# Attention and a two-layer product on one core: where x is divided by its row sums, two decoding buffers, and a second decoding tied to named steps

## The chip, the cores and the metric

The kernel runs on one NeuronCore of a Trainium2 chip. The metric is device time in microseconds (us) of one execution; the shown time of a kernel is the median of its runs. TensorE (PE) multiplies matrices, VectorE (DVE) and ScalarE (ACT) work elementwise, GpSimd (POOL) reduces over partitions, and SyncE (SP) issues most of the transfers, in the order of its program: an instruction that waits on SP holds back every transfer behind it.

## The reference, cut to what matters

```python
def phi(x):                                   # q, k: 8 batches x 8 heads x 576 x 64
    proj = einsum('bhsd,df->bhsf', x, w_phi)  # 128 features
    proj = proj - max(abs(proj), axis=-1, keepdims=True)
    return concatenate([exp(proj), exp(-proj)], axis=-1)
kv  = einsum('bhsf,bhsd->bhfd', phi(k), v)
z   = sum(phi(k), axis=2)
num = einsum('bhsf,bhfd->bhsd', phi(q), kv)
den = einsum('bhsf,bhf->bhs', phi(q), z)[..., None] + 1e-06
x   = (num / den) as 4608 tokens x 512
out = ((x @ w_a) * (x @ w_b)) @ w_out         # w_a, w_b: 512x1536, w_out: 1536x512
```

All is float32. `num / den` is the division in question: one reciprocal per head and position, multiplied into the 64 columns of its head.

## The kernel before, in words

Attention goes over 32 units, a batch b (0 to 7) and a pair of heads pr (0 to 3) each, named `b_pr`. A unit is cut into steps (project, features, products, ...), and a plan spreads the steps over turns, four turns to a unit (`attention_steps`). Up to turn 40 the units run alone; there the weights of the first six slices of the hidden size are decoded beside them (`load_weights`: a packed 64-bit word becomes a high and a low float32 part; ACT makes `w` at L427, DVE shifts and adds at L430 to L440). A new `w` tile takes the buffer of the last one, alternating between two places while units run alone, and one place later.

From turn 41 on, blocks of the two-layer product run between the steps of attention (`moe_block`): 12 blocks of T1 = 384 tokens over the first six slices, so three blocks to two batches. x of a block is read as four chunks c of 128 rows, the rows of head pair c. Each is split into a high and a low part (`x_make`). The block's first output goes to DRAM (`part`). The last four blocks run after attention has ended. Beside them the rest of the weights is decoded a second time and turned into the sums that the second pass needs (`load_factors`: raw, then `w`, `w32`, the sums `ws`, the splits `wf`), and stored. Then the second pass does the other six slices with a scheme that uses seven products for eight (`FACTORS`) over 6 blocks of T2 = 768 tokens.

The order of PE's matmuls is fixed in the order of the code while attention runs (`pe`, a manual dependency from each to the next). On the other engines the order in the program is set by a scheduler that places an instruction when its own estimate says that it is ready; `issue_after` (and `behind`) puts an instruction no earlier than a named one on the same engine.

The lines around the change: `num_products` copies the numerator of a unit to `x32` (L289). `reciprocals` (L307 to L329) stores the row sums of the unit to DRAM (`den`), loads them as a 128x9 tile `r` (L315), takes the reciprocal (L317), stores that (`rec`, L319), loads it back spread over 64 partitions per head (`rb`, two transfers, L323), multiplies (L326) and stores the result (`xnorm`, L328). `x_chunk` (L500) loads a block's chunks from `xnorm`.

Of the kernel before, what the change touches and what calls it, by code (L numbers as in the profile page):

```python
# [38 lines left out]

FACTORS, AHEAD = ("w11", "w12", "s2", "s1", "s3", "w22", "s4"), 3.2  # L40
BLOCKS_LAST = 4
# [3 lines left out]
def tile_kernel(ctx, tc, qP, km, kr, vm, vr, w_phi, eye, w_a, w_b, w_out, out):  # L45
# [33 lines left out]
    rec = [dpool.tile([H, S], F32, name=f"rec{b}") for b in range(B)]  # L79
    xnorm = [dpool.tile([DM, S], F32, name=f"xnorm{b}") for b in range(B)]  # L80
    part = dpool.tile([DM, NT], F32, name="part")
# [61 lines left out]
    def split(hi, lo, src, eng_hi, eng_lo):  # L143

        (eng_hi.copy if eng_hi is nc.scalar else eng_hi.tensor_copy)(hi, src)  # L145
        eng_lo.tensor_tensor(lo, src, hi, op=ALU.subtract)  # L146

# [130 lines left out]
    def num_products(b, pr, a1, a2, consts, st):  # L278
        u = f"{b}_{pr}"
        kvh, eq = st["kvh", b, pr], st["eq", b, pr]  # L280
        pn = duo(f"pn_{u}")
        for t in range(2):
            for s in range(2):
                for j in range(2):
                    mm(pn[heads[j], t, :HALF], kvh[:, s, heads[j]], eq[:, j, s, times[t]], start=(s == 0), stop=(s == 1))
        i = b * NPAIR + pr
        place, bufs = (alone["early"], 2) if i in EARLY_X else (a2, 4)
        x32 = st["x", b, pr] = place.tile([P, S], F32, tag="x32", bufs=bufs, name=f"x32_{u}")
# [18 lines left out]
    def reciprocals(b, pr, a1, a2, st):  # L307

        n = 2 * S // P
        hs, rows = slice(2 * pr, 2 * pr + 2), slice(pr * P, (pr + 1) * P)  # L310
        one = st["dn", b, pr].rearrange("(g r) n -> g r n", r=P // 4)[:, 0]
        behind(loads, lambda: nc.sync.dma_start(den[b][hs].rearrange("h (t n) -> (h t) n", t=2), one))
        yield
        r = a2.tile([P, n], F32, tag="rec", name=f"r_{b}_{pr}")
        behind(loads, lambda: nc.sync.dma_start(r, den[b][hs].rearrange("h (a n) -> (h a) n", n=n)))  # L315
        yield
        behind(marks, lambda: nc.vector.reciprocal(r, r))  # L317
        yield
# [12 lines left out]
    def attention_steps(pools, consts, st):
# [11 lines left out]
        for i in range(B * NPAIR):  # L343
# [66 lines left out]
    def load_weights(units, a1):  # L410
# [33 lines left out]
    def load_factors(q, nm, stage, places, pool):  # L444
# [20 lines left out]
        for k, w32 in factors.items():  # L465
# [33 lines left out]

    def x_chunk(p, j, c, pool, bufs, tag="x32"):  # L500

        T, u = TS[p], f"{p}_{j}"
        x32 = pool.tile([P, T], F32, tag=tag, bufs=bufs, name=f"x32_{u}_{c}")
        t = j * T
        while t < (j + 1) * T:
            b, s0 = divmod(t, S)
            n = min(S - s0, (j + 1) * T - t)
            nc.sync.dma_start(x32[:, t - j * T : t - j * T + n], xnorm[b][c * P : (c + 1) * P, s0 : s0 + n])
            t += n
        return x32  # L510

    def x_make(p, j, c, x32, pool):
        hl = [pool.tile([P, TS[p]], F32R, tag=f"x{k}", bufs=NCC, name=f"x{k}_{p}_{j}_{c}") for k in "hl"]
        split(*hl, x32, nc.scalar, nc.vector)
        block_x.setdefault(j, {})[c] = hl

    def first_block_x():

        for c in range(NCC):
            with tc.issue_after(loads[-1].ins):  # L520
                x32 = x_chunk(0, 0, c, xpool, 2)
            yield
            with tc.issue_after(acts[-1].ins), tc.issue_after(marks[-1].ins):
                x_make(0, 0, c, x32, xpool)
            yield

    def moe_block(p, j):
        T, pool, hpool = TS[p], xpools[0], xpools[1]
        if j not in block_x:
# [15 lines left out]
        for f in range(NFS[p]):  # L545
# [38 lines left out]
        for cc in range(NCC):  # L584
            if loaded and cc < 2:
                for c in (2, 3) if cc == 0 else (0, 1):
                    x_make(p, j + 1, c, loaded[c], pool)
            outputs(cc, range(NFS[p] - 1 if cc < ahead else 0, NFS[p]))
            acc = accs[cc]
            o = hpool.tile([P, T], F32, tag="o", bufs=2, name=f"o_{p}_{j}_{cc}")  # L590
            nc.scalar.copy(o, acc)  # L591
            nc.sync.dma_start(dst[:, cc], o)
            yield

    def factors_of_x(j, pool, xs):
# [5 lines left out]
        for c in range(half):  # L601
            x32 = pool.tile([P, 2, T2], F32, tag="x32", bufs=2, name=f"x32_1_{j}_{c}")
            x[c], x[c + half] = x32[:, 0], x32[:, 1]
            t = j * T2
            while t < (j + 1) * T2:
                b, s0 = divmod(t, S)
                m, t0 = min(S - s0, (j + 1) * T2 - t), t - j * T2
                rows = xnorm[b].rearrange("(i c p) s -> p c i s", i=2, p=P)[:, c, :, s0 : s0 + m]
                load = lambda: (nc.sync if j else nc.sync).dma_start(x32[:, :, t0 : t0 + m], rows)
# [333 lines left out]
    with ExitStack() as c:  # L943
# [107 lines left out]
```

## Time and profile before

| what | us |
|---|---|
| median of 3 runs (1176.81 to 1181.11) | 1179.69 |
| profiled execution, its own time | 1176.17 |
| span of its trace | 1174.4 |
| PE busy | 1143.0 |
| DVE busy | 735.4 |
| ACT busy | 559.2 |

The span is what the trace covers, the rest of the profiled execution's time, 1.8 us, lies around it. The granted clock of TensorE is the full one, 2.4 GHz, in nearly all of the span. The shares of busy time are means over stages of different kind: units alone to about 112 us, units beside blocks to about 540 us, blocks beside the second decoding and blocks by themselves to about 770 us, then the second pass.

### The profile page before, as it was taken

To read this page: it belongs to the slowest core of one execution; us is meant where nothing else is said; L and a number is where in the kernel's file an instruction comes from. 1 tells how busy PE (TensorE), PEld (TensorE's weight loads), DVE (VectorE), ACT (ScalarE), POOL (GpSimd) and SP (SyncE) were. 2 spreads that over 40 slices of the span, in tenths; PEclk is the share of its full clock that TensorE was granted. 3 is DMA by queue.
4 is the path that set the end of the run, shared out by engine and by line. 5 is a ranking of instruction groups with operands and counts; after the bars stand their busy time and mean duration, and the time that the engine had idled before them with its cause. 6 is when DMAs were issued, how large, how long until landed. Compare 5 with 4: busy or idle time off the path is not lost.

```text
span 1174.4 us, 21007 instructions
## 1 busy us (share of the span) xinstructions
PE 1143.0 (97%) x8198; PEld 1028.1 (88%) x8198; DVE 735.4 (63%) x1359; ACT 559.2 (48%) x1050; POOL 140.0 (12%) x69
## 2 busy tenths in 40 slices
PE   8999999999999999999999999999999999999998
PEld 6666777787888788789999999999999999999998
DVE  6886886454554546453898122647687685958675
ACT  6886675454444535443555222435344353425332
POOL 4542323122121212110000000000000000000000
PEclk9999999999999999999999999999999999999999
DMA  5566654333241423224895110067695866768582
GB/s 194 178 205 202 191 170 135 102 92 119 68 145 56 124 83 106 67 83 152 292 289 193 54 55 27 23 190 270 190 323 173 277 217 221 265 193 290 175 259 83
DMA packets 103076, 191.76 MB, mean 163 GB/s; under 512 B 19520, under 2 KB 54720, under 8 KB 102976
## 3 DMA queue, kind: packets, MB, share of 16 engines
q1 hardware_dynamic: 100080, 180.84, 48.0%
q10 hardware_dynamic: 2896, 9.57, 2.5%
q8 instruction: 65, 1.06, 0.4%
q14 instruction: 35, 0.29, 0.1%
HBM read 150.75 MB, written 39.62 MB: 162 GB/s over the span
## 4 chain that ended last, share of the span: by engine, by line
PE 76%; DVE 9%; DMA 9%; ACT 3%; issue 2%; SPq 0%; DVEq 0%; ACTq 0%
PE po L782 11%; PE pa L671 10%; PE pa L105 10%; PE po L105 10%; PE pb L105 9%; PE pb L671 9%; PE kv L105 5%; PE pn L105 4%; PE pq L105 3%; DMA rb<-rec 3%; PE pd L105 2%; DMA rec<-r 2%; PE pk L105 1%; DMA x<-xnorm 1%; DMA raw_a<-in_w_a 1%
## 5 line engine op out<-in xcount | busy, mean ns | idle before, releaser
L218 POOL PARTITION_ALL_REDUCE mb<-p x64 | 139.7, 2228 | 362.8 <-ACT p L213 358.9
L105 PE MATMUL pa<-xh,w_a 128*128 128x384 f32 x576 | 162.0, 342 | 0.6 <-DVE h L560 0.4
L105 PE MATMUL pb<-xh,w_b 128*128 128x384 f32 x576 | 158.8, 337 | 2.6 <-ACT o L591 2.0
L105 PE MATMUL po<-hh,w_o 128*128 128x384 f32 x576 | 154.9, 342 | 1.4 <-ACT hh L145 0.9
L105 PEld LDWEIGHTS po<-hh,w_o 128*128 128x128 f32 x576 | 105.4, 190 | 7.9 <-issue 3.4
L105 PEld LDWEIGHTS pa<-xh,w_a 128*128 128x128 f32 x576 | 105.1, 188 | 8.2 <-issue 3.7
L105 PEld LDWEIGHTS pb<-xh,w_b 128*128 128x128 f32 x576 | 105.1, 188 | 3.5 <-ACT o L591 2.6
L105 PE MATMUL po<-hl,w_o 128*128 128x384 f32 x288 | 97.3, 338 | 2.0 <-DVE hl L146 2.0
L560 DVE TENSOR_TENSOR h<-pb,h 128x384 f32<-128x384 f32 x72 | 39.8, 552 | 92.0 <-PE pb L105 92.0
L105 PE MATMUL pb<-xl,w_b 128*128 128x384 f32 x288 | 96.8, 336 | 0.0
L105 PE MATMUL pa<-xl,w_a 128*128 128x384 f32 x288 | 96.8, 336 | 0.0
L180 DVE TENSOR_REDUCE m<-pk 128x8 f32<-128x1024 f32 x32 | 39.1, 1220 | 86.3 <-PE pk L105 86.3
L782 PE MATMUL po<-hh_s,own_o 128*128 128x384 f32 x288 | 80.1, 336 | 0.8 <-ACT u L770 0.7
L145 ACT CAST hh<-h 128x384 fp32r<-128x384 f32 x72 | 36.8, 512 | 73.7 <-DVE h L560 73.1
L105 PE MATMUL pn<-eq,kvh 128*64 128x288 f32 x512 | 67.9, 407 | 3.6 <-DVE kvh L276 3.5
L591 ACT COPY o<-po 128x384 f32<-128x384 f32 x48 | 22.5, 477 | 85.1 <-PE po L105 73.3
L105 PE MATMUL kv<-e,v 128*64 128x256 f32 x512 | 62.3, 385 | 0.7 <-ACT e L184 0.5
L105 PEld LDWEIGHTS pn<-eq,kvh 128*64 128x64 f32 x512 | 37.2, 137 | 27.9 <-ACT eq L226 2.9
L782 PE MATMUL po<-hh_w,own_o 128*128 128x384 f32 x216 | 58.9, 335 | 0.0
L559 ACT COPY h<-pa 128x384 f32<-128x384 f32 x72 | 34.2, 475 | 51.5 <-PE pa L105 48.1
L105 PEld LDWEIGHTS po<-hl,w_o 128*128 128x128 f32 x288 | 54.7, 190 | 2.2 <-DVE hl L146 2.2
L105 PE MATMUL pq<-q,w 64*128 64x288 f32 x256 | 48.1, 451 | 8.1 <-ACT p L201 7.2
(257 smaller groups left out, 2617.1 us busy)
## 6 DMA issues: line engine op xcount, KB each, us to landing
back_s<-kept_s SPq DMA_DIRECT2D x71, 512.0 KB
back_w<-kept_w SPq DMA_DIRECT2D x52, 512.0 KB
q<-in_qP SPq DMA_DIRECT2D x32, 288.0 KB
rb<-rec SPq DMA_DIRECT2D x64, 144.0 KB
xnorm<-x SPq DMA_DIRECT2D x32, 288.0 KB
part<-o SPq DMA_DIRECT2D x48, 192.0 KB
o<-part SPq DMA_DIRECT2D x24, 384.0 KB
out_x<-o SPq DMA_DIRECT2D x48, 192.0 KB
```

Source lines behind the costliest of these rows:

```text
L105: issue = lambda: nc.tensor.matmul(out, w, x, start=start, stop=stop, skip_group_check=True)
L145: (eng_hi.copy if eng_hi is nc.scalar else eng_hi.tensor_copy)(hi, src)
L180: nc.vector.tensor_reduce(out=m, in_=p, op=ALU.max, axis=AX.X, apply_absolute_value=True)
L218: nc.gpsimd.partition_all_reduce(mb, p32[:, j], P, bass_isa.ReduceOp.absmax)
L559: nc.scalar.copy(h32, pab["a"])
L560: nc.vector.tensor_tensor(h32, pab["b"], h32, op=ALU.mult)
L591: nc.scalar.copy(o, acc)
L671: in_turn(lambda: nc.tensor.matmul(acc[to][i], w_, x_, skip_group_check=True, **at), True)
L782: in_turn(lambda: nc.tensor.matmul(acc[m, to], w_, h_, skip_group_check=True, **f), False)
```

## The change

`reciprocals` ends with the store of the reciprocals. The undivided numerator is stored to `xraw` by a step of its own (`x_store`, a turn after the products). `x_chunk` loads a chunk of it and, as `rb`, the reciprocals of the same tokens; `x_scale` multiplies and stores the result to `xnorm` for the second pass, whose tensors are now one for each of its blocks. The chunks of the next block are loaded at slices 1 and 3 of a block and scaled at slices 3 and 5. The first block's chunks follow in turns (6, 9) after the end of the shortened list of turns. `w` of the first decoding has two buffers throughout. The second decoding takes 2.2 steps for each step of a block instead of 3.2, each step behind the last low part (`hl`) or output copy (`o`) of a block, and `kept` has four buffers for five.

```diff
-REC_TURNS0, REC_TURNS, X_TURNS = (1, 3, 5, 6, 8, 10, 10), (0, 1, 3, 4, 5, 6, 6), (5, 8)
-EARLY_X = (0, 2, 4)
+REC_TURNS0, REC_TURNS, X_TURNS = (1, 3, 5, 6), (0, 1, 3, 4), (6, 9)
...
-FACTORS, AHEAD = ("w11", "w12", "s2", "s1", "s3", "w22", "s4"), 3.2
+FACTORS, AHEAD = ("w11", "w12", "s2", "s1", "s3", "w22", "s4"), 2.2
...
+    def x_store(b, pr, a1, a2, consts, st):
+        behind(loads, lambda: nc.sync.dma_start(xraw[b][pr * P : (pr + 1) * P, :], st["x", b, pr]))
...
         behind(loads, lambda: nc.sync.dma_start(rec[b][hs].rearrange("h (a n) -> (h a) n", n=n), r))
-        yield
-        rb = a2.tile([P, S], F32, tag="rb", bufs=1, name=f"rb_{b}_{pr}")
-        for j in range(2):
-            behind(loads, lambda: nc.sync.dma_start(rb[heads[j]], rec[b][2 * pr + j : 2 * pr + j + 1].broadcast_to([D, S])))
-        yield
-        x32 = st["x", b, pr]
-        behind(marks, lambda: nc.vector.tensor_tensor(x32, x32, rb, op=ALU.mult))
-        yield
-        behind(loads, lambda: nc.sync.dma_start(xnorm[b][rows], x32))
         yield
...
-            place = alone["early"] if alone["turn"] < TURNS * ALONE - 8 and len(weights) % 2 else a1
-            w = place.tile([P, 2 * DM], F32, tag="w", name=f"w_{u}")
+            w = a1.tile([P, 2 * DM], F32, tag="w", bufs=2, name=f"w_{u}")
...
-                t = pool.tile([P, 2, n], F32R, tag="kept", bufs=5, name=f"wf_q{q}_{nm}_{k}")
+                t = pool.tile([P, 2, n], F32R, tag="kept", bufs=4, name=f"wf_q{q}_{nm}_{k}")
...
+    def x_chunk(j, c, pool, tag="x32"):
+
+        x32 = pool.tile([P, T1], F32, tag=tag, bufs=2, name=f"x32_0_{j}_{c}")
+        rb = xpool.tile([P, T1], F32, tag="rb", bufs=2, name=f"rb_{j}_{c}")
+        t = j * T1
+        while t < (j + 1) * T1:
             b, s0 = divmod(t, S)
...
+            nc.sync.dma_start(x32[:, t0 : t0 + n], xraw[b][c * P : (c + 1) * P, s0 : s0 + n])
+            for i in range(2):
+                one = rec[b][2 * c + i : 2 * c + i + 1, s0 : s0 + n]
+                nc.sync.dma_start(rb[heads[i], t0 : t0 + n], one.broadcast_to([D, n]))
             t += n
...
+    def x_scale(j, c, x32, rb):
+        nc.vector.tensor_tensor(x32, x32, rb, op=ALU.mult)
+        jj, t0 = divmod(j * T1, T2)
+        nc.sync.dma_start(xnorm[jj][c * P : (c + 1) * P, t0 : t0 + T1], x32)
...
-            split(hh, hl, h32, nc.scalar, nc.vector)
+            passed.append(split(hh, hl, h32, nc.scalar, nc.vector))
             hs.append((hh, hl))
-            if f == 2 and j + 1 < blocks[0]:
-                loaded = [x_chunk(p, j + 1, c, pool, 2) for c in range(2)]
+            if f == 1 and j + 1 < blocks[0]:
+                loaded = [x_chunk(j + 1, c, pool) for c in range(2)]
+            if f in (3, 5) and loaded:
+                for c in (0, 1) if f == 3 else (2, 3):
+                    x_scale(j + 1, c, *loaded[c])
             if f == 3 and loaded:
-                loaded += [x_chunk(p, j + 1, c, hpool, 2, "o") for c in range(2, NCC)]
+                loaded += [x_chunk(j + 1, c, hpool, "o") for c in range(2, NCC)]
...
             acc = accs[cc]
             o = hpool.tile([P, T], F32, tag="o", bufs=2, name=f"o_{p}_{j}_{cc}")
-            nc.scalar.copy(o, acc)
+            passed.append(nc.scalar.copy(o, acc))
...
             while due >= 1:
-                next(ahead, None)
+                with tc.issue_after(passed[-1].ins):
+                    next(ahead, None)
                 due -= 1
```

On DVE, where unit 2_1 takes the maximum of its features (`m`) and the exponents' argument (`d`); `kvh` is what PE multiplies next, and `x32` the numerator. Before:

```order
L180 TENSOR_REDUCE m_2_1_1165<-pk_2_1_1155 128x8
L181 TENSOR_TENSOR d_2_1_1164<-pk_2_1_1155,m_2_1_1165 128x1024
L317 RECIPROCAL r_1_1_1122<-r_1_1_1122 128x9
L440 TENSOR_TENSOR w_0_2_b_1087<-w_0_2_b_1057 128x512
L276 COPY kvh_1_3_1191<-pt_1_3_1187 128x384
L326 TENSOR_TENSOR x32_1_0_831<-x32_1_0_831,rb_1_0_1147 128x576
L219 TENSOR_TENSOR p32_2_1_1150<-p32_2_1_1150,mb_2_1_0_1175 128x576
```

And now:

```order
L180 TENSOR_REDUCE m_2_1_1179<-pk_2_1_1169 128x8
L507 TENSOR_TENSOR x32_0_1_0_1643<-x32_0_1_0_1643,rb_1_0_1644 128x384
L181 TENSOR_TENSOR d_2_1_1178<-pk_2_1_1169,m_2_1_1179 128x1024
L318 RECIPROCAL r_1_1_1131<-r_1_1_1131 128x9
L431 TENSOR_TENSOR w_0_2_b_1094<-w_0_2_b_1070 128x512
L276 COPY kvh_1_3_1205<-pt_1_3_1201 128x384
L507 TENSOR_TENSOR x32_0_0_3_1159<-x32_0_0_3_1159,rb_0_3_1160 128x384
L219 TENSOR_TENSOR p32_2_1_1164<-p32_2_1_1164,mb_2_1_0_1189 128x576
```

The multiply of unit 1_0 stood behind `kvh` of unit 1_3. Now the multiply of block 1's chunk 0 (`x32_0_1_0`, half of whose tokens are unit 1_0's) stands ahead of `d_2_1` and of that `kvh`. The next one, of chunk 1, stands right ahead of `m_2_2`.

On SP at the same place, from the store of the reciprocals of unit 1_0 to the loads that its multiply needs (`r` are the row sums as loaded, `den` as stored). Before:

```order
L319 DMA rec1_77<-r_1_0_985 128x9
L328 DMA xnorm0_84<-x32_0_3_699 128x576
L508 DMA x32_0_0_2_1126<-xnorm0_84 128x384
L168 DMA rv_2_2_1251<-in_vr 128x256
L323 DMA rb_1_0_1147<-rec1_77 64x576 x2
L312 DMA den1_69<-dn_1_2_1139 4x288
```

And now:

```order
L320 DMA rec1_77<-r_1_0_995 128x9
L316 DMA r_1_1_1131<-den1_69 128x9
L509 DMA xnorm0_92<-x32_0_0_2_1019 128x384
L168 DMA rv_2_2_1257<-in_vr 128x256
L502 DMA rb_1_0_1644<-rec0_76 64x192 x2
L502 DMA rb_1_0_1644<-rec1_77 64x192
L290 DMA xraw1_85<-x32_1_2_1105 128x576
L499 DMA x32_0_1_0_1643<-xraw0_84 128x192
L499 DMA x32_0_1_0_1643<-xraw1_85 128x192
L313 DMA den1_69<-dn_1_2_1150 4x288
L502 DMA rb_1_0_1644<-rec1_77 64x192
```

Two loads of `rb` have become four, and between the two that read `rec1` stand a store, two loads and the store of the next unit's row sums.

On DVE beside block 7, between its slices 1 and 2 (`h32` a product of a slice, `hl` its low part; names with `q` are the second decoding). Before:

```order
L560 TENSOR_TENSOR h32_0_7_1_6171<-pb_0_7_1_6158,h32_0_7_1_6171 128x384
L461 TENSOR_TENSOR ws_q1_b_6991<-ws_q1_b_6991,w32_q1_b_6908 128x256
L462 TENSOR_TENSOR ws_q1_b_6991<-w32_q1_b_6908,ws_q1_b_6991 128x256
L390 TENSOR_SCALAR w_q2_a_0_7105<-w_q2_a_0_7105 128x512
L146 TENSOR_TENSOR hl_0_7_1_6175<-h32_0_7_1_6171,hh_0_7_1_6174 128x384
L392 TENSOR_SCALAR w_q2_a_0_7105<-w_q2_a_0_7105 128x512
L146 TENSOR_TENSOR wf_q1_b_s2_7043<-ws_q1_b_6991,wf_q1_b_s2_7043 128x256
```

And now:

```order
L562 TENSOR_TENSOR h32_0_7_1_6233<-pb_0_7_1_6220,h32_0_7_1_6233 128x384
L146 TENSOR_TENSOR hl_0_7_1_6237<-h32_0_7_1_6233,hh_0_7_1_6236 128x384
L562 TENSOR_TENSOR h32_0_7_2_6276<-pb_0_7_2_6263,h32_0_7_2_6276 128x384
L146 TENSOR_TENSOR hl_0_7_2_6280<-h32_0_7_2_6276,hh_0_7_2_6279 128x384
L562 TENSOR_TENSOR h32_0_7_3_6309<-pb_0_7_3_6296,h32_0_7_3_6309 128x384
```

The instructions of the second decoding that follow the last slice of block 6, 7, 8, 9, 10 and 11, and so stand beside the outputs of that block or the next block's slices, number 62 in block 6, 56 in 7, 20 in 8, none in 9, 1 in 10 and 29 in 11 before, counted from the first slice of each, and 0, 0, 40, 41, 40 and 49 now.

## Rows read from the trace of the kernel before

**Rows 1.** The page: busy time, share, instructions; then the chain that ended last.
```profile
PE 1143.0 (97%) x8198; PEld 1028.1 (88%) x8198; DVE 735.4 (63%) x1359; ACT 559.2 (48%) x1050; POOL 140.0 (12%) x69
...
PE 76%; DVE 9%; DMA 9%; ACT 3%; issue 2%; SPq 0%; DVEq 0%; ACTq 0%
```

**Rows 2.** Windows: stretch, length, then busy time and instructions of each engine.
```profile
120.00:200.00 80.00, 73.90 (x725) 57.86 (x725) 62.15 (x104) 51.11 (x82) 22.00 (x10) 0.98 0.55 166
200.00:540.00 340.00, 335.84 (x2569) 279.37 (x2566) 169.24 (x263) 163.49 (x266) 69.18 (x32) 1.00 0.32 96
540.00:640.00 100.00, 96.30 (x544) 93.65 (x543) 83.67 (x194) 51.24 (x121) 0.00 (x0) 1.00 0.76 251
640.00:770.00 130.00, 129.34 (x746) 129.05 (x746) 42.92 (x93) 40.92 (x91) 0.00 (x0) 1.00 0.17 53
```

**Rows 3.** Waits of PE, 60 to 125 us: total us, times, longest.
```profile
PE pn L105 <- DVE kvh L276: 3.2, 4, 1.1
PE pt L274 <- ACT dn L300: 1.1, 1, 1.1
```

**Rows 4.** Line L326, the multiply: its instructions; what ended the idle time before them.
```profile
L326 DVE TENSOR_TENSOR x<-x,rb x32: 696/748/1685, 49.7 to 541.6; 128x576 f32<-128x576 f32 x32
...
  DMA rb<-rec: 20.1, 9
```

**Rows 5.** Chain of waits, 60 to 110 us: start, us, what.
```profile
61.76 5.92 DMA rec<-r
...
72.59 3.90 DMA rec<-r
...
77.05 3.94 DMA rb<-rec
...
82.94 5.17 DMA rec<-r
...
88.68 2.93 DMA rb<-rec
```

**Rows 6.** Timeline of DVE, 76 to 106 us: start, us, instruction, idle before and releaser.
```profile
79.60 0.20 DVE L317 RECIPROCAL r<-r 128x9 f32<-128x9 f32 x1
81.08 0.76 DVE L326 TENSOR_TENSOR x<-x,rb 128x576 f32<-128x576 f32 x1 [1.27 <-DMA rb<-rec]
...
86.81 1.23 DVE L181 TENSOR_TENSOR d<-pk,m 128x1024 f32<-128x1024 f32 x1
...
88.62 0.55 DVE L276 COPY kvh<-pt 128x384 f32<-128x384 f32 x1
91.63 0.76 DVE L326 TENSOR_TENSOR x<-x,rb 128x576 f32<-128x576 f32 x1 [2.46 <-DMA rb<-rec]
...
96.24 1.22 DVE L180 TENSOR_REDUCE m<-pk 128x8 f32<-128x1024 f32 x1
...
98.63 0.55 DVE L276 COPY kvh<-pt 128x384 f32<-128x384 f32 x1
```

**Rows 7.** Timeline of PE, 144 to 153 us.
```profile
148.94 0.76 PE L105 MATMUL pq<-q,w 64*128 64x288 f32 x4 [3.08 <-ACT p L201]
```

**Rows 8.** Timelines of ACT, 144 to 153 us and 176 to 184 us.
```profile
146.19 0.66 ACT L427 ACTIVATE w_o<-raw_o 128x512 f32<-128x512 f32 x1 [2.24 <-DVE w_b L440]
...
148.26 0.63 ACT L201 COPY p<-pq 128x576 f32<-128x576 f32 x1
...
180.78 0.66 ACT L427 ACTIVATE w_o<-raw_o 128x512 f32<-128x512 f32 x1 [1.86 <-DVE w_o L440]
```

**Rows 9.** Waits of DVE, 200 to 540 us.
```profile
DVE m L180 <- PE pk L105: 74.1, 11, 9.7
```

**Rows 10.** Waits of PE, 200 to 540 us.
```profile
PE po L105 <- DVE hl L146: 2.0, 1, 2.0
```

**Rows 11.** Chain of waits, 540 to 640 us.
```profile
544.63 3.41 DMA raw_a<-in_w_a
...
568.59 2.05 DMA x<-xnorm
```

**Rows 12.** Waits of ACT, 540 to 640 us.
```profile
ACT w_q_a L389 <- DMA raw_a<-in_w_a: 9.5, 3, 5.4
```

More of the change, by code (lines that the diff above doesn't have):

```diff
@@ L79, in tile_kernel @@
     rec = [dpool.tile([H, S], F32, name=f"rec{b}") for b in range(B)]
-    xnorm = [dpool.tile([DM, S], F32, name=f"xnorm{b}") for b in range(B)]
+    xraw = [dpool.tile([DM, S], F32, name=f"xraw{b}") for b in range(B)]
+    xnorm = [dpool.tile([DM, T2], F32, name=f"xnorm{j}") for j in range(NT // T2)]
     part = dpool.tile([DM, NT], F32, name="part")
@@ L145, in split @@
         (eng_hi.copy if eng_hi is nc.scalar else eng_hi.tensor_copy)(hi, src)
-        eng_lo.tensor_tensor(lo, src, hi, op=ALU.subtract)
+        return eng_lo.tensor_tensor(lo, src, hi, op=ALU.subtract)
     heads = [slice(j * D, (j + 1) * D) for j in range(2)]
@@ L285, in num_products @@
                     mm(pn[heads[j], t, :HALF], kvh[:, s, heads[j]], eq[:, j, s, times[t]], start=(s == 0), stop=(s == 1))
-        i = b * NPAIR + pr
-        place, bufs = (alone["early"], 2) if i in EARLY_X else (a2, 4)
-        x32 = st["x", b, pr] = place.tile([P, S], F32, tag="x32", bufs=bufs, name=f"x32_{u}")
+        x32 = st["x", b, pr] = a2.tile([P, S], F32, tag="x32", name=f"x32_{u}")
         nc.scalar.copy(x32.rearrange("p (t n) -> p t n", t=2), pn[:, :, :HALF])
+    def x_store(b, pr, a1, a2, consts, st):
+        behind(loads, lambda: nc.sync.dma_start(xraw[b][pr * P : (pr + 1) * P, :], st["x", b, pr]))
     def den_products(b, pr, a1, a2, consts, st):
@@ L309, in reciprocals @@
         n = 2 * S // P
-        hs, rows = slice(2 * pr, 2 * pr + 2), slice(pr * P, (pr + 1) * P)
+        hs = slice(2 * pr, 2 * pr + 2)
         one = st["dn", b, pr].rearrange("(g r) n -> g r n", r=P // 4)[:, 0]
@@ L352, in attention_steps @@
             units = ((project, 0), (q_features, TURNS), (turned_kv, 0), (summed, 0), (kv_products, 0), (num_products, 0), (z_products, 0), (kv_out, 0))
-            units += ((den_products, 0), (load_kq, -5), (load_v, -2 if i else 0))
+            units += ((den_products, 0), (load_kq, -5), (load_v, -2 if i else 0), (x_store, at["num_products"] + 1))
             for order, (f, t) in enumerate(units):
@@ L358, in attention_steps @@
             done = t0 + at["den_products"]
-            plan(10, reciprocals(b, pr, *pools, st), [done + t for t in rec_turns])
+            plan(len(units), reciprocals(b, pr, *pools, st), [done + t for t in rec_turns])
             if b == 0:
-                plan(11, x_first, [done + rec_turns[-1] + t for t in X_TURNS])
+                plan(len(units) + 1, x_first, [done + rec_turns[-1] + t for t in X_TURNS])
             if pr == NPAIR - 1:
-                plan(12, b, [done + rec_turns[-1]])
+                plan(len(units) + 2, b, [done + rec_turns[-1]])
         stages.sort(key=lambda x: x[:3])
@@ L498, in weight, with x_make @@
         return weights[key][:, i]
[L500 to L505, printed above, removed]
-            b, s0 = divmod(t, S)
-            n = min(S - s0, (j + 1) * T - t)
-            nc.sync.dma_start(x32[:, t - j * T : t - j * T + n], xnorm[b][c * P : (c + 1) * P, s0 : s0 + n])
-            t += n
-        return x32
-    def x_make(p, j, c, x32, pool):
-        hl = [pool.tile([P, TS[p]], F32R, tag=f"x{k}", bufs=NCC, name=f"x{k}_{p}_{j}_{c}") for k in "hl"]
+    def x_chunk(j, c, pool, tag="x32"):
[3 more added lines that the diff above has]
+        while t < (j + 1) * T1:
+            b, s0 = divmod(t, S)
+            n, t0 = min(S - s0, (j + 1) * T1 - t), t - j * T1
+            nc.sync.dma_start(x32[:, t0 : t0 + n], xraw[b][c * P : (c + 1) * P, s0 : s0 + n])
+            for i in range(2):
+                one = rec[b][2 * c + i : 2 * c + i + 1, s0 : s0 + n]
+                nc.sync.dma_start(rb[heads[i], t0 : t0 + n], one.broadcast_to([D, n]))
+            t += n
+        return x32, rb
+    def x_scale(j, c, x32, rb):
+        nc.vector.tensor_tensor(x32, x32, rb, op=ALU.mult)
+        jj, t0 = divmod(j * T1, T2)
+        nc.sync.dma_start(xnorm[jj][c * P : (c + 1) * P, t0 : t0 + T1], x32)
+    def x_make(j, c, x32):
+        hl = [xpool.tile([P, T1], F32R, tag=f"x{k}", bufs=NCC, name=f"x{k}_0_{j}_{c}") for k in "hl"]
         split(*hl, x32, nc.scalar, nc.vector)
@@ L520, in first_block_x @@
             with tc.issue_after(loads[-1].ins):
-                x32 = x_chunk(0, 0, c, xpool, 2)
+                chunk = x_chunk(0, c, xpool)
             yield
             with tc.issue_after(acts[-1].ins), tc.issue_after(marks[-1].ins):
-                x_make(0, 0, c, x32, xpool)
+                x_scale(0, c, *chunk)
+                x_make(0, c, chunk[0])
             yield
@@ L530, in moe_block @@
             with tc.issue_after(loads[-1].ins):
-                chunks = deque(x_chunk(p, j, c, pool, 2) for c in range(2))
+                chunks = deque(x_chunk(j, c, pool) for c in range(2))
             yield
@@ L586, in moe_block @@
                 for c in (2, 3) if cc == 0 else (0, 1):
[L587 removed]
+                    x_make(j + 1, c, loaded[c][0])
             outputs(cc, range(NFS[p] - 1 if cc < ahead else 0, NFS[p]))
@@ L603, in factors_of_x @@
             x[c], x[c + half] = x32[:, 0], x32[:, 1]
[L604 to L609, printed above, removed]
+            for t in range(0, T2, T2 // 2):
+                rows = xnorm[j].rearrange("(i c p) s -> p c i s", i=2, p=P)[:, c, :, t : t + T2 // 2]
+                load = lambda: nc.sync.dma_start(x32[:, :, t : t + T2 // 2], rows)
                 behind(feeds, load) if j else load()
-                t += m
                 yield
@@ L881, in home @@
         return wpool, f"w_{f}_{nm}"
-    kept, begun, feeds = {}, set(), []
+    kept, begun, feeds, passed = {}, set(), [], []
     weights, pools_moe, xpools, block_x, blocks, marks, acts, copies, loads, alone = {}, [], [xpool], {}, [0], [], [], [], [], dict(turn=0)
```

6 lines of the change are left out of this document (4 added, 2 removed).

## The prediction

> **What bounds the kernel now.** I read the page first, to see which engine is nearly always busy: PE, with 1143.0 of 1174.4 us [rows 1]. What a change can win is therefore the 31 us in which PE stands still, and what it can lose is new standstill. The shares of the chain that ended last say the same (76% PE, 9% DVE, 9% DMA). Next come the windows [rows 2]: each stage has its own loss. From 640 to 770 us, blocks by themselves, 746 matmuls take 130 us, 0.1743 us each; from 540 to 640 us, beside the second decoding, only 544 run in 100 us, which at that pace need 94.8 us, so 5.2 us are lost there. The second pass is touched only in how it loads x, so I leave it at its present time. Then the waits of PE by stage: near the end of the units alone it waits 3.2 us for the copy `kvh` on DVE and 1.1 us for `dn` on ACT [rows 3]; between 125 and 200 us it waits twice for a copy of p on ACT, 6.0 us together, of which one is 3.08 us [rows 7]. Last I asked who holds DVE: the multiply by `rb` has 20.1 us of idle time before it, in 9 waits for DMA [rows 4], and the chain from 61.8 us on runs through the store of `rec` and the load of `rb` [rows 5].
>
> The sum is made against the profiled execution, 1176.17 us. It lies 3.5 us under the median of the runs shown, 1179.69 us, and the forecast adds that back. What a measurement of this kernel can tell from no change I take as 0.5%, 5.9 us: below 1173.8 us is faster, above 1185.6 us slower.
>
> **Part 1, the division moves from the unit to the block.** DVE's own work hardly changes: 32 multiplies of 0.748 us (median) go [rows 4], 48 over 384 columns come, which by their columns take 0.50 us each: 23.9 against 24.0 us. SP gets 107 more transfers. They are off the path except where SP itself waits, which is what matters here. In the order DVE's multiply of block 1's chunk 0 now stands ahead of `d_2_1`, and of the `kvh` that PE stalls for already. It needs `rec1` of unit 1_0, so the store and load that the change takes out of the unit come back here. Working from the rows: before, the waits at 81.08 and 91.63 us cost DVE 1.27 and 2.46 us [rows 6]. Without the first, and with 1.0 us won already at the wait before it (PE's longest stall for `kvh` is 1.1 us [rows 3]), the reciprocal at 79.60 comes at about 78.6 and its store goes out at about 79. The store takes 3.9 to 5.9 us to land, 5.0 in the mean of three [rows 5], so SP goes on at 84. Between the two loads that read it stand four issues of about half a microsecond, so the second goes out at 86 and lands 2.9 to 3.9 us later [rows 5], at about 89.3. DVE reaches the multiply at about 85.3 (`d` at 86.81 before, 1.5 us earlier now): it waits 4.0 us. Then 0.5 for the multiply, 1.2 for `d` and 0.8 for what stands between bring `kvh` to 91.8 us instead of 88.62 [rows 6], 3.2 us late. What is queued behind this wait is what PE needs next, `kvh` of unit 1_3, and `d`, which ACT waits for. The second multiply, chunk 1 ahead of `m_2_2`: from 91.8 on DVE has 0.55 of `kvh`, 0.5 of a multiply and the 3.9 us of work that lay between the end of the multiply at 92.4 and `m` at 96.24 [rows 6], so it is there at 96.8; the reciprocal it needs comes behind `d` at 91.0, its store lands at 96.1, two issues and 3.5 us more make 100.4: a wait of 3.6 us. With multiply, `m` and `d` (3.0 us) `kvh` of unit 2_0 starts at 103.4, against 98.63 before: 4.8 us late. What goes in return is the stall for `dn` behind the last of these waits, 1.1 us [rows 3]. **+3.7 us.** If both legs are at their shortest each wait is 1.6 us less: about +0.5. With the longest they are about 1 us more: +5.7. If DVE's slack swallows both, the stalls of rows 3 go: −4.3.
>
> The Trainium skill, DMA: Bandwidth & Descriptors, section Anatomy of one DMA, puts a small transfer at a fixed part of about 2.0 us, fitted on transfers that GpSimd issues. By that price, an estimate, the two legs would be 4 us and neither multiply would wait, and this part would be −4.3 and the whole sum 8 us lower. The trace disagrees for the 4.5 KB store at this place, with 3.90 to 5.92 us.
>
> Later blocks' multiplies stand where their units ended longer ago, so they wait only for the chunk's own loads, 2.05 us for a chunk of x and up to 3.94 for `rb` by the nearest rows [rows 5, 11]. DVE has idle time there, 74.1 us before `m` from 200 to 540 us, up to 9.7 at once [rows 9], and PE loses little in that stage now: 335.84 of 340 us busy [rows 2]. But a late `hl` has cost PE 2.0 us once [rows 10]. From 0 to 5 us; nearer to the row of idle time: **+1.5 us.**
>
> **Part 2, two buffers for `w`.** ACT makes the next `w` only when DVE has added up the last: it stands 2.24 us at 146.19 and 1.86 us at 180.78, and the copy of p that PE waits for is behind it, at 148.26 in the first case [rows 7, 8]. With a second buffer both go; what is late next is PE's own last product for that copy. **−4.1 us**, between 0 (the next cast waits for DVE in its place) and −6.0 (both stalls whole).
>
> **Part 3, the second decoding.** Counted in the order it leaves blocks 6 and 7 (62 and 56 instructions on DVE) and stands with 40, 41, 40 and 49 in blocks 8 to 11. A block has 216 matmuls, 37.6 us. At DVE's mean in 540 to 640 us, 83.67 / 194 = 0.43 us [rows 2], a block of 41, with its own 12 for `h32` and `hl` and 8 for x, is 61 x 0.43 = 26 us, 70% of the block; before, DVE was busy for 84% of this stage. PE's loss of 5.2 us should fall to about 2: **−3.2 us**, between −5.2 and +2. Block 11 now has 49, 26 of them after its last slice, beside 72 matmuls of outputs (12.5 us): 11.2 us of DVE. It fits narrowly, with ACT's casts and the loads of raw words beside it: **+1.5 us**, 0 to 6. The four buffers for five of `kept` lie beside the same work and are in these bounds.
>
> One row moves the other way: on ACT the first two `w` of the second decoding now stand ahead of the output copy `o` of block 5, chunk 3, and wait for a load of raw words. Such a load takes 3.41 us in the chain, and ACT waited for it 9.5 us in 3 waits, up to 5.4 [rows 11, 12]. Behind it on ACT stand the copies that free PE's accumulators. 0 to 5.4; the load is issued well ahead, so **+1.0 us.**
>
> **Sum:** +3.7 +1.5 −4.1 −3.2 +1.5 +1.0 = +0.4 us, so 1176.6 us on the profiled scale and 1180 us on the median's.
>
> **The rivals.** A, the waits are simply gone: DVE's slack hides both early multiplies, later ones never wait, and what rows 3, 4 and 7 show is won. −4.3, −4.1 and, for the second decoding with block 11 fitting, −3.7: −12.1 us, 1168 us. For it: DVE is only 63% busy. Against: PE stalls for `kvh` already, behind the very waits that come back. By the Trainium skill's price for a small transfer, above, this is the outcome; the rows speak against its price, not against slack.
>
> B, the multiply that waits stands in DVE's order ahead of what PE needs. Alone it costs +5.7, and beside the blocks a third of the 20 to 24 later multiplies cost PE 1 us each, +7; with −4.1, −3.2, +1.5 and +1.0 as above that is +7.9: 1188 us. For it: three of the stage's present stalls are of this make, and the loads of a chunk are issued late behind SP's own waits. Against: 74.1 us of idle time. It decides from about 4.8 us of new waiting of PE: that is what the other parts win, and from 10.7 us the slowdown can be told.
>
> C, the second decoding comes too late: block 11's sums and their stores are not ready when the second pass wants them. +6 there, and −1 instead of −3.2 before: +7.1, 1187 us. For it: the rows of block 11 fill its last part to nine tenths. Against: 62 instructions stood behind block 6 before at a loss of only a few microseconds.
>
> **How the numbers follow.** The forecast, no change that can be told, 0.38; A 0.32; B 0.20; C 0.10. So faster 0.32, same 0.38, slower 0.30. The forecast's own range is 1174 to 1186 us. The range for 8 in 10 reaches to A's and past B's time: 1167 to 1190 us; its lower end is 12.7 us under the median, with parts 1 and 2 both at their best.
>
> **What would show it.** The multiply at L507 waits about 4 us for `rb` at 85 us and again at 97 us, and `kvh` of unit 2_0 is late by 4 to 5 us (if it comes early, A). PE's stalls of 3 us for p near 149 and 183 us are gone or under 1 us. Between 540 us and the second pass PE's pace is 112 or more matmuls in 20 us in every window. PE's waits from 200 to 540 us stay under 6 us in sum; over 10, B. The forecast is wrong if the alone stage comes out ahead of before, or if DVE or ACT hold the outputs of block 11 for more than 4 us.

## The result and the profile after

The changed kernel takes 1188.64 us (1187.46 to 1192.29, 6 runs) against 1179.47 us beside it: a ratio of 1.0083, 95% interval 1.0063 to 1.0103. It is slower by 9.2 us. The profiled execution's span went from 1174.4 to 1185.9 us. In the page of the changed kernel PE is busy for 2.8 us more than before [rows 1]; most of what grew is the time around it:

```profile
PE 1145.8 (97%) x8198; PEld 1028.8 (87%) x8198; DVE 746.9 (63%) x1375; ACT 560.1 (47%) x1050; POOL 139.4 (12%) x69
```

The order of PE's products is nearly the same in both kernels, so the start of the same product in two traces says how far one has fallen behind. The table gives it for the changed kernel and for those of the next section: us later than before (less than zero: ahead). Each column is one execution, and that of the kernel before took 3.3 us less than its median.

| place (start in the trace of before) | changed | hold1 | hold_all | hold_w1 | undo2 | undo3 | b_part3 |
|---|---|---|---|---|---|---|---|
| pn of unit 1_2 (79.0) | -1.9 | -1.5 | -1.3 | -1.1 | -1.1 | -0.9 | 0.3 |
| pn of unit 2_0 (99.3) | 8.6 | -2.2 | -2.0 | -1.9 | 8.3 | 7.6 | 0.6 |
| block 0 (111.7) | 10.9 | 1.6 | 3.0 | -2.1 | 9.4 | 10.1 | 0.9 |
| pn of unit 7_0 (472.5) | 17.3 | 7.5 | 2.0 | -5.2 | 11.5 | 17.8 | 3.1 |
| block 9 (652.8) | 12.8 | 3.0 | -3.4 | -10.6 | 7.0 | 19.8 | -3.2 |
| end of the last product (1170.5) | 11.9 | 2.6 | -4.9 | -13.0 | 7.4 | 23.2 | -2.9 |

So 10.9 us are lost before block 0, some 6 more beside the blocks, and 5 to 6 come back beside the second decoding. The first loss is in the waits of PE from 60 to 125 us, where [rows 3] had 3.2 and 1.1:

```profile
PE pn L105 <- DVE kvh L276: 10.7, 3, 7.1
PE pt L274 <- ACT dn L301: 1.8, 1, 1.8
```

DVE's timeline of the changed kernel, 76 to 112 us, answers to [rows 6]. The two early multiplies (L507) wait 5.54 and 4.28 us, and `kvh` starts at 92.72 and 107.26 where it started at 88.62 and 98.63. The releasers in the brackets are the last to come by the profile; the load of `k` was issued behind the last load of `rb`.

```profile
90.44 0.56 DVE L507 TENSOR_TENSOR x<-x,rb 128x384 f32<-128x384 f32 x1 [5.54 <-DMA k<-in_km]
...
92.72 0.55 DVE L276 COPY kvh<-pt 128x384 f32<-128x384 f32 x1
...
98.75 0.69 DVE L429 TENSOR_TENSOR w_a<-w_a 128x512 f32<-128x512 f32 x1 [1.96 <-ACT w_a L426]
...
104.39 0.56 DVE L507 TENSOR_TENSOR x<-x,rb 128x384 f32<-128x384 f32 x1 [4.28 <-DMA x<-xraw]
...
107.26 0.55 DVE L276 COPY kvh<-pt 128x384 f32<-128x384 f32 x1
```

On SP the store of `rec` went out at 79.18. The two loads of `rb` that went out from 82.65 on read the reciprocals of batch 0; SP had stood there 1.5 us for the load of `q`. The third, which reads what the store wrote, went out at 84.37, 5.2 us behind it, and the last that the first multiply needs at 87.15, behind a store, two loads and a store. The row of 84.37 and the wait come from views of their own:

```profile
79.18 0.38 SPq L320 DMA_DIRECT2D rec<-r  x1
...
82.65 2.17 SPq L502 DMA_DIRECT2D rb<-rec  x3
84.92 0.59 SPq L290 DMA_DIRECT2D xraw<-x  x1
85.60 0.93 SPq L499 DMA_DIRECT2D x<-xraw  x2
86.58 0.52 SPq L313 DMA_DIRECT2D den<-dn  x1
87.15 0.45 SPq L502 DMA_DIRECT2D rb<-rec  x1
```
```profile
84.37 0.45 SPq L502 DMA_DIRECT2D rb<-rec  x1
...
SPq L502 <- DMA q<-in_qP: 1.5, 1, 1.5
```

The windows of the same stretch show a second price, in the column after POOL's, the granted clock: after PE has stood for most of 86 to 93 us it runs at 0.50, 1.2 GHz, for 4 us, and the 16 products of `pn` take 4.11 us. Before, `pn` took 2.16 (the last row).

```profile
86.00:93.00 7.00, 0.32 (x4) 0.00 (x0) 2.56 (x5) 1.17 (x2) 2.58 (x2) 0.84 0.57 169
93.00:95.00 2.00, 1.59 (x8) 0.97 (x10) 1.64 (x4) 2.00 (x4) 0.00 (x0) 0.50 0.85 231
95.00:97.00 2.00, 2.00 (x12) 0.94 (x8) 1.75 (x4) 0.13 (x1) 0.00 (x0) 0.50 0.83 280
```
```profile
93.41 4.11 PE L105 MATMUL pn<-eq,kvh 128*64 128x288 f32 x16 [7.09 <-DVE kvh L276]
...
107.95 3.75 PE L105 MATMUL pn<-eq,kvh 128*64 128x288 f32 x16 [3.14 <-DVE kvh L276]
```
```profile
89.31 2.16 PE L105 MATMUL pn<-eq,kvh 128*64 128x288 f32 x16 [1.06 <-DVE kvh L276]
```

Over the whole kernel the multiply's line has this idle time before it, where [rows 4] had 20.1 for `rb`; some of it lies where DVE had nothing else to do:

```profile
L507 DVE TENSOR_TENSOR x<-x,rb x48: 543/558/1734, 61.0 to 719.0; 128x384 f32<-128x384 f32 x48
...
  DMA x<-xraw: 50.5, 19
```

PE's waits from 125 to 215 us are 2.3 us for p in three, where the kernel before had 6.0 in two, one of them [rows 7], but there is a new one of 3.2 for DVE's sums of `w`. From 558 to 658 us, the stretch that answers to the third row of [rows 2], PE runs 579 matmuls, and 746 in the 130 us behind:

```profile
PE po L105 <- DVE w_o L431: 3.2, 1, 3.2
PE pq L105 <- ACT p L201: 2.3, 3, 2.0
```
```profile
558.00:658.00 100.00, 100.00 (x579) 100.00 (x578) 37.78 (x77) 31.79 (x67) 0.00 (x0) 1.00 0.33 107
658.00:788.00 130.00, 129.34 (x746) 129.05 (x745) 101.35 (x231) 62.34 (x148) 0.00 (x0) 1.00 0.64 216
```

### The profile page after: what moved, and what is told of

Read it like the earlier page. It is cut to its first block, busy times and chain, and to the rows that moved or that the text cites. A ratio compares the mean times of both kernels' runs of the same rounds, so it can differ in the third digit from the quotient of the medians.

```text
span 1185.9 us, 21181 instructions
## 1 busy us (share of the span) xinstructions
PE 1145.8 (97%) x8198; PEld 1028.8 (87%) x8198; DVE 746.9 (63%) x1375; ACT 560.1 (47%) x1050; POOL 139.4 (12%) x69
## 4 chain that ended last, share of the span: by engine, by line
PE 75%; DVE 7%; DMA 4%; ACT 1%; issue 1%; SPq 0%; ACTq 0%; DVEq 0%
PE pa L105 12%; PE po L105 12%; PE pb L105 12%; PE po L783 10%; PE pa L672 9%; PE pb L672 8%; PE kv L105 5%; PE pn L105 3%; PE pd L105 2%; PE pq L105 2%; DMA back_s<-kept_s 1%; DMA x<-xnorm 1%; PE pk L105 1%; DVE top L684 1%; DMA rec<-r 1%
## 5 line engine op out<-in xcount | busy, mean ns | idle before, releaser
L507 DVE TENSOR_TENSOR x<-x,rb 128x384 f32<-128x384 f32 x48 | 29.6, 622 | 98.5 <-DMA x<-xraw 50.5
L105 PE MATMUL pn<-eq,kvh 128*64 128x288 f32 x512 | 71.5, 423 | 12.0 <-DVE kvh L276 11.9
L105 PE MATMUL kv<-e,v 128*64 128x256 f32 x512 | 65.0, 398 | 2.1 <-ACT e L184 2.1
L105 PEld LDWEIGHTS kv<-e,v 128*64 128x64 f32 x512 | 35.0, 141 | 24.2 <-issue 7.4
```

Source lines behind the costliest of these rows:

```text
L105: issue = lambda: nc.tensor.matmul(out, w, x, start=start, stop=stop, skip_group_check=True)
```

## The experiments

Theory D: the multiply stands too early in DVE's order. Its rival S: SP's longer queue holds everything up. Theory P3 and its rival N are on the second decoding, W on the second buffer of `w`, K on the clock. Each time is a median, with the ratio to the kernel before on the same chip. Each edit is scheduled anew, so other rows can move with the one that it names; where that bears on a reading, it is said.

**hold1, hold_all: the multiplies held where the code has them**, those of block 1, then of all blocks.

```diff
                 for c in (0, 1) if f == 3 else (2, 3):
-                    x_scale(j + 1, c, *loaded[c])
+                    with tc.issue_after(passed[-1].ins) if j == 0 else nullcontext():   # hold_all: always
+                        x_scale(j + 1, c, *loaded[c])
```

> The changed kernel with the four multiplies of block 1's chunks held behind the low part (hl) of the slice that they stand behind in the code; all transfers stay where they are. Theory D (the multiply stands in DVE's order ahead of kvh and waits there for rec and rb): the drift of 10.5 us between units 1_2 and 2_0 goes, PE reaches block 0 no later than before, and the time is 1174 to 1179 us. Rival S (SP: 107 more transfers and the waits between them hold back every load): the transfers are unchanged, so the time stays at 1186 to 1190 us.

> As the run before, with the multiplies of all blocks held so. Theory D: a further 3 to 7 us, the drift between 120 and 510 us, so 1169 to 1175 us. Rival S: 1186 to 1190 us.

1178.86 us (1.001, 0.9988 to 1.0031) and 1171.09 us (0.9945, 0.9925 to 0.9965). Both times are as D has it. The early multiplies cost 9.8 us by the medians, 8.6 by the ratios, the later ones 7.8. In the table the drift at unit 2_0 turns from +8.6 to -2.2. Against S stands the first wait: up to the load of `q` that follows the last load of `rb`, SP issues the same transfers in the same order in hold1, and `pn` of unit 1_3 behind it starts 1.4 us earlier than before, where it started 4.1 us later in the changed kernel. Further on hold1 moves transfers too, since loads of `rb` and stores to `xnorm` wait for the held multiplies, and there the two theories are not parted.

What the later multiplies cost is not all waiting for their loads. Of the 5.5 us between hold1 and hold_all at unit 7_0, 4.6 come at one place. In hold1 `hl` stands on DVE behind four splits (`xl`) of the next block's x, PE waits 1.96 us for it, and then the clock falls and `kv` takes 3.68 us. In hold_all the multiplies, and so these splits, come behind `hl`, and the wait is 0.15. First hold1, then hold_all:

```profile
394.60 1.02 DVE L146 TENSOR_TENSOR xl<-x,xh 128x384 fp32r<-128x384 f32 x2
395.54 0.55 DVE L146 TENSOR_TENSOR hl<-h,hh 128x384 fp32r<-128x384 f32 x1
...
396.14 0.69 PE L105 MATMUL po<-hl,w_o 128*128 128x384 f32 x1 [1.96 <-DVE hl L146]
...
397.08 3.68 PE L105 MATMUL kv<-e,v 128*64 128x256 f32 x16
```
```profile
392.73 0.56 DVE L146 TENSOR_TENSOR hl<-h,hh 128x384 fp32r<-128x384 f32 x1
393.21 1.02 DVE L507 TENSOR_TENSOR x<-x,rb 128x384 f32<-128x384 f32 x2
...
393.35 0.45 PE L105 MATMUL po<-hl,w_o 128*128 128x384 f32 x1 [0.15 <-DVE hl L146]
```

The kernel before has the same wait for `hl` [rows 10]. So with this wait hold_all wins something that the change had not lost.

**undo3, b_part3: the second decoding as before in the changed kernel; as now in the kernel before.**

```diff
-FACTORS, AHEAD = ("w11", "w12", "s2", "s1", "s3", "w22", "s4"), 2.2
+FACTORS, AHEAD = ("w11", "w12", "s2", "s1", "s3", "w22", "s4"), 3.2
...
-                with tc.issue_after(passed[-1].ins):
-                    next(ahead, None)
+                next(ahead, None)
```

> The changed kernel with 3.2 steps of the second decoding to a step of a block and not behind named steps, as in the kernel before. Theory P3 (spreading the second decoding over four blocks wins the 6 us by which PE catches up from 540 us on): 1193 to 1196 us, and PE falls short of its pace after block 5 again. Rival N (what is caught up there comes from elsewhere, the decoding being hidden either way): 1187 to 1190 us.

> The kernel before with only the second decoding changed: 2.2 steps behind the named steps, four buffers of kept. Theory P3: 6 us faster than before, 1172 to 1175 us. Rival N: 1178 to 1181 us.

1197.39 us (1.0162, 1.0122 to 1.0202), 1.4 us over the expected range, and 1175.34 us (0.9975, 0.9953 to 0.9997), 0.3 us over it and 2.7 under N's. P3 stands by the table between unit 7_0 and block 9. undo3 loses a further 3.4 us behind block 9, which the kernel before does not; it keeps the four buffers of `kept`, and whether they are why was not tested. The windows, undo3 first, then b_part3: 530 matmuls in 100 us against 579.

```profile
557.00:657.00 100.00, 93.74 (x530) 91.29 (x530) 80.50 (x185) 47.26 (x111) 0.00 (x0) 1.00 0.80 269
```
```profile
540.00:640.00 100.00, 100.00 (x579) 100.00 (x578) 31.45 (x63) 30.70 (x65) 0.00 (x0) 1.00 0.22 74
```

In b_part3 the 6.3 us won between unit 7_0 and block 9 stand against 3.1 lost before that. Of these 2.8 are lost at one place, behind a wait for `hl` of 1.95 us that the kernel before has too (1.96, [rows 10]); there the clock stayed at 1.00, here it fell. First the kernel before, then b_part3:

```profile
391.94 1.95 PE L105 MATMUL kv<-e,v 128*64 128x256 f32 x16
...
390.00:395.00 5.00, 3.60 (x30) 2.34 (x32) 2.79 (x5) 0.48 (x1) 0.00 (x0) 1.00 0.38 124
```
```profile
391.72 0.69 PE L105 MATMUL po<-hl,w_o 128*128 128x384 f32 x1 [1.95 <-DVE hl L146]
...
392.66 3.68 PE L105 MATMUL kv<-e,v 128*64 128x256 f32 x16
...
390.00:395.00 5.00, 3.28 (x14) 1.90 (x16) 3.12 (x6) 0.48 (x1) 0.00 (x0) 0.57 0.36 118
```

At the same wait the changed kernel loses 1.7 us and undo2 nothing. So up to 2.8 us of a column of the table can hang on whether the clock falls there; what decides it no run shows.

**hold_w1, hold_prelu, undo2, hold_w1_prelu: the second buffer of `w`.** hold_w1 and undo2 give it up in hold_all and in the changed kernel. The prelu kernels keep ACT's first step of every decoding behind the copies of kv and dn.

```diff
-            w = a1.tile([P, 2 * DM], F32, tag="w", bufs=2, name=f"w_{u}")
+            place = alone["early"] if alone["turn"] < TURNS * ALONE - 8 and len(weights) % 2 else a1
+            w = place.tile([P, 2 * DM], F32, tag="w", name=f"w_{u}")
...
-        nc.scalar.copy(back, st["kv", b, pr])
+        copies.append(nc.scalar.copy(back, st["kv", b, pr]))   # prelu; dn likewise
...
-            with tc.issue_after(acts[-1].ins):
+            with tc.issue_after(acts[-1].ins), tc.issue_after(copies[-1].ins) if copies else nullcontext():   # prelu
```

> hold_all with the first decoding's w as before (one buffer, alternating places while the units run alone). Theory W0 (two buffers trade ACT's wait for DVE's last addition against a wait for the raw words, so they win next to nothing): 1169 to 1173 us beside hold_all's 1171.1; PE's two waits for p near 145 and 180 us come back, and its wait of 4.5 us for dn near 106 us goes. Rival W4 (the 4 us of part 2 are really won): 1174 to 1177 us.

> hold_all with ACT's first step of a decoding (the one that waits for raw words) held behind the last copies of kv and dn in the code. Theory W0: what stands behind ACT's wait for raw words at 101 to 104 us is dn, which PE wants; held behind it, PE's 4.5 us wait for dn goes and the time is 1166 to 1169 us. Rival: PE waits there for something else that is as late (DVE's kvh or the cast), 1170 to 1173 us.

> The changed kernel with w of the first decoding as before, the early multiplies left where they are. Theory W (the second buffer lets ACT take the next raw words ahead of back and dn, where it waits for their load; it cost 7 us beside the held multiplies): 1180 to 1185 us, and PE's wait for dn before block 0 is under 1 us. Rival W4 (with the multiplies in the way the second buffer pays, since DVE's sums come late there): 1190 to 1194 us, and PE's two waits for p of 3 us are back.

> hold_w1 with ACT's first step of a decoding behind the last copies of kv and dn. Theory W: that step no longer stands ahead of dn with one buffer, so this changes little: 1162 to 1166 us. Rival (its 2.0 us wait for raw words near 104 us still costs PE): 1160 to 1162 us.

hold_w1 1164.11 us (0.988, 0.9863 to 0.9896), hold_prelu 1166.48 us (0.9894, 0.9875 to 0.9912), undo2 1182.11 us (1.0029, 1.001 to 1.0049), hold_w1_prelu 1164.68 us (0.9889, 0.987 to 0.9909). hold_w1 lies 5 us under the range of either theory: the second buffer does not win little, as W0 had it, but costs 7.0 us beside the held multiplies and 6.5 beside the early ones. ACT's and PE's timelines of hold_all show how most of it comes there:

```profile
104.12 0.66 ACT L418 ACTIVATE w_a<-raw_a 128x512 f32<-128x512 f32 x1 [3.04 <-DMA raw_a<-in_w_a]
...
105.57 0.50 ACT L301 ACTIVATE dn<-pd,eps 128x288 f32<-128x288 f32 x1
```
```profile
106.12 0.55 PE L274 MATMUL pt<-ident,back 128*128 128x128 f32 x3 [4.53 <-ACT dn L301]
```

With a free buffer ACT's step was placed ahead of `back` and `dn`, and waits there for raw words. In hold_w1 the same step stands behind `dn`, and PE's wait there is 0.91 us:

```profile
102.69 0.55 PE L274 MATMUL pt<-ident,back 128*128 128x128 f32 x3 [0.91 <-ACT dn L301]
```

hold_prelu's edit holds only such steps, though DVE's order moves with them, and wins 4.6 of the 7.0 us. With one buffer the same hold wins nothing. In the table 5.1 us of the buffer's price beside the held multiplies lie ahead of block 0. Beside the early ones only 1.5 of 5.8 at unit 7_0 do, and 1.7 are the clock at the wait for `hl`; how the rest comes was not followed.

**rb_old: no round trip of the reciprocals for block 1.**

```diff
-                one = rec[b][2 * c + i : 2 * c + i + 1, s0 : s0 + n]
+                one = rec[0 if j == 1 else b][2 * c + i : 2 * c + i + 1, s0 : s0 + n]
```

> The changed kernel with the reciprocals of block 1 all read from batch 0's tensor, which was written long before; every instruction of DVE up to the two early multiplies and every transfer stays at its place, but nothing waits for the store of rec of units 1_0 to 1_3 any more (half of block 1 is then divided by the wrong sums). Theory D-rt (the round trip of the reciprocals through DRAM is the wait of both multiplies): the wait of 5.5 us is under 1.5 us, the wait of 4.3 us under 2 us, the time 1179 to 1183 us. Rival D-x (the chunk's own numerators, stored and loaded again, come as late): both waits stay over 3 us, 1186 to 1190 us.

1184.02 us (1.0047, 1.0032 to 1.0062), 4.6 us faster, between the two. The waits fell from 5.54 and 4.28 to 3.53 and 3.28:

```profile
89.07 0.56 DVE L507 TENSOR_TENSOR x<-x,rb 128x384 f32<-128x384 f32 x1 [3.53 <-DMA rb<-rec]
...
102.03 1.67 DVE L507 TENSOR_TENSOR x<-x,rb 128x384 f32<-128x384 f32 x1 [3.28 <-issue]
```

The landing of `rec` is at least 1 to 2 us of each; before the second, SP still stood 1.8 us for that store, at its store of the numerators:

```profile
SPq L290 <- DMA rec<-r: 1.8, 1, 1.8
```

The rest is SP's own row of issues: with nothing to wait for in `rec`, the first of its three loads went out at 80.67 and the last that the first multiply needs still at 86.07, behind the store and loads of numerators. So S has a part in the wait, but only because a multiply stands where the wait is felt.

**rb_one, hold_w1_rb1: one transfer for both heads.**

```diff
-            for i in range(2):
-                one = rec[b][2 * c + i : 2 * c + i + 1, s0 : s0 + n]
-                nc.sync.dma_start(rb[heads[i], t0 : t0 + n], one.broadcast_to([D, n]))
+            both = rec[b][2 * c : 2 * c + 2, s0 : s0 + n].unsqueeze(1).broadcast_to([2, D, n])
+            nc.sync.dma_start(rb[:, t0 : t0 + n], both)
```

> The changed kernel with one transfer for both heads' reciprocals of a piece instead of two, 28 fewer rows on SP; the early multiplies still stand ahead of kvh. Theory D (place on DVE): at most 3 us faster, 1185 to 1189 us, since the multiply still waits for rec to land. Rival S (SP's queue): 1179 to 1184 us.

> hold_w1 with one transfer for both heads' reciprocals. Theory D: the multiplies are behind their data already, so fewer transfers win nothing: 1162 to 1166 us. Rival S: SP's transfers still hold PE up beside the blocks, 1158 to 1161 us.

1236.84 us (1.0507, 1.0485 to 1.0529) and 1226.3 us (1.0415, 1.039 to 1.0441): neither theory, and no test of S. The transfer itself is slow. hold_w1_rb1's chain of waits from 540 us on has it at 10.15 us, and while it moves, the share of busy DMA engines and GB/s (the last two columns) are:

```profile
573.16 10.15 DMA rb<-rec
```
```profile
575.00:577.00 2.00, 2.00 (x14) 2.00 (x13) 0.44 (x1) 0.00 (x0) 0.00 (x0) 1.00 0.09 31
577.00:579.00 2.00, 2.00 (x13) 2.00 (x13) 0.78 (x3) 0.51 (x1) 0.00 (x0) 1.00 0.14 47
```

**fill1: PE kept at work in its longest wait.**

```diff
         pn = duo(f"pn_{u}")
+        for n_ in range({(1, 3): 40}.get((b, pr), 0)):
+            mm(pn[heads[n_ % 2], 0, :HALF], consts[1][:, heads[n_ % 2]], eq[:, 0, 0, times[0]])
```

> The changed kernel with 40 more matmuls (64 columns of the identity against eq) written into the accumulator pn of unit 1_3 just before its own first product overwrites them, so that PE works through most of its 7.1 us wait for kvh; they need 5.4 us at the pace of that product. Theory K (the wait costs more than its length: after it PE runs at 1.2 GHz, and the 16 products of pn take 4.11 us instead of 2.16): the granted clock stays at 1.0, these 16 take 2.2 us, unit 2_0's product starts about 2 us earlier than in the changed kernel, and the time is 1186 to 1188 us. Rival (the slow products are due to late weights, not to the clock): they take 4 us again, and the time stays at 1188 to 1190 us.

1191.29 us (1.01, 1.0076 to 1.0123): slower than expected by either, though not clear of the changed kernel. The rows that it was made for are clear. The fill took 9.87 us, not 5.4, and so overran the wait, but the clock stayed at 1.00 and the 16 products of `pn` took 2.11 us instead of 4.11:

```profile
87.29 9.87 PE L105 MATMUL pn<-eq,ident 128*64 128x288 f32 x80
96.99 2.11 PE L105 MATMUL pn<-eq,kvh 128*64 128x288 f32 x16
...
106.20 2.11 PE L105 MATMUL pn<-eq,kvh 128*64 128x288 f32 x16
...
115.09 0.90 PE L274 MATMUL pt<-ident,back 128*128 128x128 f32 x3 [4.58 <-ACT dn L303]
115.92 3.68 PE L105 MATMUL kv<-e,v 128*64 128x256 f32 x16
```

So the slow products are the clock's, as K has it. That unit 2_0's product came 1.75 us earlier is not shown to be: `pn` of unit 1_3 ended 1.6 us later than in the changed kernel. What came earlier is the second multiply, by 2.46 us, and SP's order ahead of it had changed with the edit: the store of unit 1_3's numerators stands ahead of the loads of `xraw` in the changed kernel and behind them in fill1. This run does not part that from the clock. First the changed kernel, then fill1:

```profile
98.54 0.42 SPq L290 DMA_DIRECT2D xraw<-x  x1
```
```profile
104.12 0.54 SPq L292 DMA_DIRECT2D xraw<-x  x1
```

The wait of 4.58 us for `dn` ended 0.6 us earlier than that of 1.80 in the changed kernel, but behind it the clock fell (`kv` 3.68 us where 1.95 is usual), and block 0 started 2.2 us later than there.

## Why the prediction was right or wrong

The measured time lies in the range, and near rival B's 1188 us; the forecast itself, no change at 1180 us, was wrong. By its steps:

- **The early multiplies, +3.7 predicted.** The mechanism was right: place, wait and what is queued behind. DVE arrived at 84.9 (85.3 said) and waited 5.54 (4.0); the second waited 4.28 (3.6). What failed is the size: by hold1 they cost 9.3 us at block 0, of the 10.9 there. Two things were left out of the term. The clock: the two slow `pn` took 2.0 and 1.6 us more than 2.16 each. And `dn`, which I had counted as a stall that goes: it grew to 1.8 us, beside the second buffer of part 2 (0.6 in undo2). The 1.96 us before L429, where ACT's cast stood behind the copy of the late `pn`, cost nothing of their own: DVE then stood 4.28 us at the second multiply.
- **The later multiplies, +1.5 (0 to 5).** 7.8 us by hold1 against hold_all (5.5 of them by unit 7_0 in the table). I took DVE's idle time before `m` as cover. B's price of +7 there was near, but its mechanism is not shown for most of it: 4.6 us are the wait for `hl` behind the splits of x and the clock behind that, a wait that the kernel before has as well.
- **The second buffer, -4.1 (0 to -6).** The sign was wrong: 6.5 to 7.0 us lost. The step that failed is "with a second buffer both go; what is late next is PE's own last product". Late next was the load of raw words, and the scheduler placed the step that waits for it ahead of `back` and `dn`. Nor did p need the buffer: in hold_w1, with one, PE's waits for p from 125 to 215 us are 2.1 us in sum.
- **The second decoding, -3.2 +1.5 +1.0.** 5.9 us won (18.7 us behind at block 6, 12.8 at block 9), and no loss in block 11: 746 matmuls in 130 us. Block 5 loses 1.4 us, but as much in undo3, where the second decoding is as before, so the cost I added for its `o` is not seen either. The costs did not come; C falls.
- **A**'s 12.1 us were to be had, but not by its terms: hold_w1 wins 14.6 with the multiplies held and one buffer of `w`. The mean granted clock goes with it, 0.999 to 1.000 in hold_w1's runs, 0.992 to 0.997 in the kernel before beside them, 0.990 to 0.993 in the changed kernel. That DVE is 63% busy over the span said nothing on the rows where it waited.

That B's total was hit is partly chance: its terms alone (+5.7) and for the second buffer (-4.1) were too good, that for the second decoding (-0.7 in sum) too bad.

The Trainium skill's fixed part of about 2.0 us (DMA: Bandwidth & Descriptors, Anatomy of one DMA) stays below what the changed kernel shows for the store of `rec`, 5.2 us from its issue to that of the load that reads it. I had counted 5.0. But by rb_old the landing was the smaller part of the first wait.

The best kernel here is hold_w1: the division in the block, its multiplies held behind the slice they belong to, one buffer of `w`, the second decoding spread. It is 24.5 us under the changed kernel and 14.6 us under the one before.

## What to carry to other kernels

When an operation moves to where a scheduler may place it freely, look where it lands in the engine's order: if it stands ahead of the critical rows with data that must make a round trip, those rows wait with it, whatever the engine's busy share. A freed buffer lets an instruction be placed earlier as well as run earlier; ask what it waits for then, and who is behind it. Hold a moved operation behind a named row of its own stage before judging the move. And before a gain is put down to an edit, look whether the kernel before has the same wait, and whether the clock fell behind it in one trace and not in the other.

## What the runs showed of the hardware

- A wait of PE costs more than its length: after 7.09 us of standing still the granted clock was 0.50 (1.2 GHz) and 16 products took 4.11 us, with filled PE 2.11 (fill1).
- A wait of the same length need not end the same way: after 1.96 us for `hl` the clock stayed at 1.00 in the kernel before, and 16 products of `kv` took 1.95 us; after 1.95 us at the same place it was 0.57 in b_part3, and they took 3.68.
- A transfer that reads two rows, each spread over 64 partitions, in one instruction moved 31 to 47 GB/s at a DMA share of 0.09 to 0.14 and took 7 to 10 us; transfers of one row took 2.9 and 3.9 us in the kernel before [rows 5]. The Trainium skill, DMA: Bandwidth & Descriptors, section Why a DMA increments its semaphore by 16 and not by 1, says that a transfer runs on as many engines, up to 16, as divide the slowest dimension of both sides. The source's is 2 here and the tile's 128 rows, so 2 of 16 engines, an estimate of 0.125 for the share: the trace agrees.
